# Attention and two gated FFNs on one core: state products on half-array rows, attention on small tiles, and x loaded by ScalarE's queue

## The chip, the core and the metric

The kernel runs on one core of a Trainium2 chip. The time is the device time of one execution in microseconds; smaller is better. Three executions before the change gave 1411.93, 1411.97 and 1413.6 us, a median of 1411.97 us. A profiled execution of the same program took 1415.93 us.

## The reference, cut to what matters

```python
# x[8, 8, 512, 64], state[8, 8, 32, 64]: batch, head, row, feature
scores = x @ state.T / 8;   a  = softmax(scores)    # rows of x over 32 state rows
xread  = a @ state
scores2 = state @ x.T / 8;  a2 = softmax(scores2)   # state rows over 512 rows of x
sread  = a2 @ x
t = concat([xread, sread], rows)      # per batch 512 + 32 rows, 8 heads x 64 = 512 columns
t = t.transpose(0, 2, 1, 3).reshape(4352, 512)
h = ((t @ w1) * (t @ w2)) @ w3 @ w_out              # 512 -> 1024 -> 1024 -> 512
y = (sigmoid(h @ w_gate) * (h @ w_val)) @ w_out2    # 512 -> 1536 -> 512
```

Everything is float32. w_gate is scaled by 200, so the argument of the sigmoid is large and the products must be precise. The weights arrive as 64-bit floats and are converted on the chip from their two 32-bit halves.

## The kernel before, in words

**Precise products.** An operand is split into two fp32r parts (a rounded one and the rest), and a product takes three matmuls: high by high, high by low, low by high (`products`, L103 to L115). The attention's own small products (scores, state read, transposes) are plain fp32 matmuls; each shows two records in the trace.

**State products.** For the 512 rows of a batch, xread @ w1 is a @ (state @ w1). The kernel computes state @ w1 and state @ w2 per head ("state products", `sw_step`, L337), stores them in DRAM (sw_d, tile swd) and reads them back per batch as weights (`sw_weights`, L458: swf is the loaded tile, swh its two parts). For this, `bd` holds the transposed state as a block diagonal: 128 rows are two heads of 64 features, and the columns of a head are zero in the other head's rows. A step multiplies one 128x512 piece of a weight (wh) with two blocks of bd's parts (bds): six matmuls of 128 rows and 512 columns into two PSUM banks (psw), two copies by ScalarE, one store. 16 steps for four of the batches stand at the start, 16 for the other four in the stages t = 1 and 2.

**Stages.** `ffn1` (L408) runs once per batch, t = 0 to 7 (the batches in the order 0, 4, 1, 5, 2, 6, 3, 7), and once more for the state rows. A stage has eight steps j (groups pab: a @ swh for w1 and w2; ScalarE copies the first to asb, VectorE multiplies, both split the result to u) and four steps d (groups py: u times wp, the product of w3 and w_out, which stage 0 computes). Before each step the functions in its slot run, in the order in which the lists are filled (L610 to L645). By them the attention of the next batch is laid into the stage:

- slots 6 and 7: four groups of transposes of x (xn to PSUM tile pxt to xT, L166 to L173);
- slot 8: the scores (tile psc), and from it both softmaxes; slot 9: the rest of the first one, which gives aT, the operand of the next stage;
- in the next stage, slots 1 and 2: transposes of the second softmax (pa2); slot 4: the state read (`sread`, tile psr, copied to sr with the normalisation); slot 6: its transposes (`sreadt`, tile psrt, copied to xst).

`load_x` (L152) issues eight DMAs, one per head, on SyncE in slot 0 of the stage (slot 7 for t = 0). Its buffer comes alternately from two pools, one buffer each. From stage 3 on, the preparation of the second FFN's weights (raw, w_gate, w_val) also stands in slots.

**What sets the order.** The order of TensorE's instructions is the order of the program (L147: `manual_schedule` for PE). The order on the other engines is made by a scheduler. PSUM has eight banks: four for pab and psw (L128), two for py, two for everything of the attention.

**The rest.** The stage of the state rows ends at 620 us; the second FFN, which the change does not touch, runs to the end.

Of the kernel before, what the change touches and what calls it, by code (L numbers as in the profile page):

```python
# [20 lines left out]
def tile_state_attention__then__gated_ffns(  # L21
# [96 lines left out]
    sw_d = dram.tile([2, 2, 2, 2, P, B // 2, 512], F32, name="swd")  # L118
# [19 lines left out]
    bd = keep.tile([P, G, B // 2, P], F32, name="bd")  # L138
# [7 lines left out]
    with tc.manual_schedule(engines={mybir.EngineType.PE}):  # L146
# [5 lines left out]
        def load_x(b, pool):  # L152
            t = pool.tile([P, G, SC, 2, D], F32, name="xn", bufs=1)
            for h in range(H):
                nc.sync.dma_start(
                    out=t[:, h // 2, :, h % 2], in_=x[b, h].rearrange("(p c) d -> p c d", c=SC)
                )
            xn[b] = t

        def attention(b):  # L160

            b2, bp = divmod(b, B // 2)
# [14 lines left out]
            def scores():  # L177
# [5 lines left out]
                for k in range(2):  # L183
                    pt = ps_at.tile([P, 512], F32, tag="at", name="psc")
                    for q in range(2):
                        nc.tensor.matmul(
                            pt[64 * q : 64 * q + 64],
                            bd[:, 2 * k + q, bp, b2 * 64 : b2 * 64 + 64],
                            t["xT"][:, 2 * k + q],
                            start=True,  # L190
                            stop=True,
                        )
                    nc.vector.transpose(out=t["st"][:, k].rearrange("p a n -> p (a n)"), in_=pt)
# [46 lines left out]
            def sread():  # L240
                pt = ps_at.tile([P, 2, P], F32, tag="at", name="psr")
                for k in range(2):
                    for c in range(SC):
                        for q in range(2):
# [7 lines left out]
                t["sr"] = at.tile([P, 2, P], F32, name="sr")  # L252
# [5 lines left out]
            def sreadt():  # L258
                pt = ps_at.tile([P, 2, 2, 2, NS], F32, tag="at", name="psrt")
                for k in range(2):  # L260
# [3 lines left out]
                xv = p2["xst"].rearrange("p (k q) n -> p k q n", q=2)  # L264
                for h2 in range(2):
                    nc.vector.tensor_copy(
                        out=xv[64 * h2 : 64 * h2 + 64, :, :, b * NS : (b + 1) * NS],
                        in_=pt[64 * h2 : 64 * h2 + 64, :, :, h2],
                    )
# [865 lines left out]
```

## Time and profile before

| quantity | value |
|---|---|
| median of three executions | 1411.97 us |
| profiled execution | 1415.93 us |
| its span, first to last instruction | 1414.2 us |
| mean granted clock of TensorE | 0.983 |
| TensorE busy | 1343.5 us, 95% |
| VectorE busy | 924.7 us, 65% |
| ScalarE busy | 750.2 us, 53% |
| GpSimd busy | 278.3 us, 20% |

Times in the profile run from the start of the span, 1.7 us less than the execution. Busy is the time in which an engine has an instruction under way; a step that stands beside others on an engine that is busy throughout is seen by the distance of its start to the next one's, not by its mean. The granted clock is 1 for full speed. The stages lie at 75 to 194.9 us (t = 0), 194.9 to 257.6, 257.6 to 321.5, 321.5 to 373.2, 373.2 to 424.9, 424.9 to 483.3, 483.3 to 535 and 535 to 586 us (t = 7), then the state rows; these bounds were read from the timeline as the first pab of each stage.

### The profile page before, as it was taken

How to read it: one execution, taken by the hardware profiler on the slowest of the kernel's cores; microseconds unless marked ns; L12 is line 12 of the kernel's file. 1: busy time of each engine (PE TensorE's matmuls, PEld its weight loads, DVE VectorE, ACT ScalarE, POOL GpSimd, SP SyncE). 2: the span in 40 equal slices, each digit the busy share in tenths (PEclk: the TensorE clock that was granted, in tenths of full speed). 3: DMA queues.
4: the chain of work that ended last, by engine and by line, in shares of the span. 5: the costliest groups of instructions: out<-in, count | busy, mean ns of one | idle time of the engine just before them, and what ended most of it. 6: DMA issues, size and time to landing. Idle time of an engine off the chain costs nothing.

```text
span 1414.2 us, 18988 instructions
## 1 busy us (share of the span) xinstructions
PE 1343.5 (95%) x6560; PEld 1145.6 (81%) x6560; DVE 924.7 (65%) x1523; ACT 750.2 (53%) x1480; POOL 278.3 (20%) x255
## 2 busy tenths in 40 slices
PE   5669999999998999999999999999999999999997
PEld 3348877777876777898988998988988888988996
DVE  6789756645555566528677667778777677556543
ACT  6877656756445456436546546545545544433421
POOL 2352113324334234001121121021121110000000
PEclk9889999999999999999999999999999999999999
DMA  9867637754446354383343347655445694134132
GB/s 264 290 195 212 199 135 230 228 195 127 138 119 164 90 155 152 118 319 116 133 151 100 117 165 285 239 183 169 136 167 184 227 324 159 62 108 137 49 104 67
DMA packets 169128, 237.18 MB, mean 168 GB/s; under 512 B 46920, under 2 KB 111944, under 8 KB 166984
## 3 DMA queue, kind: packets, MB, share of 16 engines
q1 hardware_dynamic: 130536, 163.15, 36.6%
q10 hardware_dynamic: 37344, 63.39, 12.8%
q0 software_dynamic: 1152, 9.44, 1.9%
q8 instruction: 51, 0.84, 0.2%
q14 instruction: 45, 0.37, 0.1%
HBM read 150.99 MB, written 84.93 MB: 167 GB/s over the span
## 4 chain that ended last, share of the span: by engine, by line
PE 80%; DVE 6%; issue 5%; DMA 4%; POOL 2%; ACT 2%; ACTq 0%; SPq 0%; DVEq 0%; POOLq 0%
PE po L1019 19%; PE psA L922 18%; PE psB L922 9%; PE pab L112 8%; PE py L112 7%; PE psC L922 5%; PE pab L115 4%; PE py L115 4%; DMA yf<-yd 2%; PE pwp L112 2%; POOL wh L66 2%; PE pwp L115 1%; PE psr L245 1%; PE pxt L170 1%; DMA raw<-in_moe_w 1%
## 5 line engine op out<-in xcount | busy, mean ns | idle before, releaser
L922 PE MATMUL psA<-y,wt 128*128 128x448 f32 (+1 forms) x1440 | 304.6, 360 | 5.6 <-ACT u L61 2.8
L922 PEld LDWEIGHTS psA<-y,wt 128*128 128x128 f32 x1440 | 266.3, 188 | 25.8 <-ACT u L61 3.9
L1019 PE MATMUL po<-wo,p 128*128 128x512 f32 x1224 | 280.7, 389 | 0.4 <-DVE p L590 0.4
L1019 PEld LDWEIGHTS po<-wo,p 128*128 128x128 f32 x1224 | 229.5, 188 | 48.3 <-DVE p L590 1.0
L922 PE MATMUL psB<-y,wt 128*128 128x448 f32 (+1 forms) x720 | 161.1, 359 | 0.0
L66 POOL TENSOR_TENSOR o<-m,o 128x256 fp32r<-128x256 f32 x72 | 59.3, 823 | 503.3 <-ACT o L61 449.1
L112 PE MATMUL pab<-aT,swh 128*128 128x512 f32 x512 | 145.7, 407 | 12.2 <-ACT asb L61 4.7
L922 PEld LDWEIGHTS psB<-y,wt 128*128 128x128 f32 x720 | 133.5, 188 | 8.5
L112 PE MATMUL py<-u,wp 128*128 128x512 f32 (+1 forms) x576 | 132.2, 381 | 2.1 <-DVE u L66 1.7
L61 ACT ACTIVATE u<-psA 128x448 f32<-128x448 f32 (+1 forms) x120 | 63.9, 532 | 127.7 <-PE psA L922 103.0
L112 PEld LDWEIGHTS py<-u,wp 128*128 128x128 f32 x576 | 104.0, 189 | 28.5 <-issue 5.7
L66 POOL TENSOR_TENSOR swh<-swf,swh 128x512 fp32r<-128x512 f32 x64 | 90.8, 1424 | 167.9 <-ACT swh L61 155.0
L112 PEld LDWEIGHTS pab<-aT,swh 128*128 128x128 f32 x512 | 95.3, 193 | 35.0 <-ACT asb L61 6.4
L61 ACT ACTIVATE p<-sg 128x448 fp32r<-128x448 f32 (+1 forms) x120 | 67.9, 566 | 86.6 <-DVE sg L958 79.0
L434 DVE TENSOR_TENSOR asb<-asb,pab 128x512 f32<-128x512 f32 (+1 forms) x72 | 47.0, 654 | 98.8 <-PE pab L115 90.3
L101 DVE CUSTOM_DVE_ANT_0 m<-m,r 128x1024 uint16<-128x1024 uint16 (+1 forms) x116 | 80.1, 692 | 11.1 <-ACT r L90 1.3
L66 DVE TENSOR_TENSOR u<-asb,u 128x512 fp32r<-128x512 f32 (+1 forms) x72 | 65.9, 916 | 30.7 <-ACT u L61 30.1
L1034 DVE TENSOR_TENSOR ob<-po,ob 128x512 f32<-128x512 f32 x68 | 46.8, 688 | 58.7 <-PE po L1019 55.4
L115 PE MATMUL pab<-aT,swh 128*128 128x512 f32 x256 | 81.7, 401 | 2.0 <-POOL swh L66 2.0
L922 PE MATMUL psC<-y,wt 128*128 128x448 f32 (+1 forms) x360 | 80.9, 360 | 1.1 <-DVE s L955 1.1
L61 ACT ACTIVATE y<-yf 128x448 fp32r<-128x448 f32 (+1 forms) x120 | 63.1, 558 | 32.4 <-DMA yf<-yd 32.4
L98 DVE SCALAR_TENSOR_TENSOR m<-raw,m 128x512 uint32<-128x512 uint32 (+1 forms) x116 | 78.2, 676 | 3.2
(118 smaller groups left out, 2028.3 us busy)
## 6 DMA issues: line engine op xcount, KB each, us to landing
raw<-in_moe_w SPq DMA_DIRECT2D x48, 512.0 KB, 5.6
wt<-wd SPq DMA_DIRECT2D x12, 1792.0 KB, 7.6
part<-ob SPq DMA_DIRECT2D x68, 256.0 KB, 2.8
ob<-part SPq DMA_DIRECT2D x68, 256.0 KB, 3.9
yf<-yd SPq DMA_DIRECT2D x37, 448.0 KB, 4.0
swd<-swst ACTq DMA_DIRECT2D x32, 512.0 KB, 4.1
swf<-swd SPq DMA_DIRECT2D x128, 128.0 KB, 3.7
wd<-o ACTq DMA_DIRECT2D x56, 256.0 KB, 2.3
```

Source lines behind the costliest of these rows:

```text
L61: return nc.scalar.activation(out=o, in_=i, func=AF.Copy)
L66: (sub or nc.vector).tensor_tensor(out=lo, in0=src, in1=hi.bitcast(F32), op=ALU.subtract)
L98: nc.vector.scalar_tensor_tensor(out=mu, in0=hi, scalar=0x80000000, in1=mu, op0=ALU.bitwise_and, op1=ALU.bitwise_or)
L101: nc.vector.tensor_tensor(out=m.bitcast(I32), in0=m.bitcast(I32), in1=r, op=ALU.add)
L112: nc.tensor.matmul(o, w[i], xx[k], start=n == 0 and i + k == 0, stop=False)
L115: nc.tensor.matmul(o, w[1 - late], xx[late], start=False, stop=n == len(pairs) - 1)
L170: nc.tensor.transpose(pt[:, c * P : (c + 1) * P], xn[b][:, g, c].rearrange("p a d -> p (a d)"), ident)
L245: nc.tensor.matmul(pt[64 * q : 64 * q + 64, k], t["a2"][:, k, c, 64 * q : 64 * q + 64], xn[b][:, 2 * k + q, c].rearrange("p a d -> p (a d) ...
L434: p2["dve"] = nc.vector.tensor_tensor(out=asb[:, :n], in0=asb[:, :n], in1=pab[1][:, :n], op=ALU.mult)
L922: nc.tensor.matmul(o, w[:, i, kb * P : (kb + 1) * P], xx[kb][h], start=start, stop=i == 1 and kb == 1, skip_group_check=True,)
L1019: nc.tensor.matmul(o, pt[j][i][:, s * P : (s + 1) * P], wot[j][:, h], start=j == js[0] and i + h == 0, stop=j == js[-1] and i == 1,)
L1034: nc.vector.tensor_tensor(out=ob, in0=o, in1=ob, op=ALU.add)
```

## The change

**State as it is.** The zero blocks go. z holds the state of four batches side by side (128 rows = 4 batches x 32), and one transpose per pair of heads turns it into stT: 64 rows per head, 128 columns for four batches. The first four batches are now 0 to 3, the order of the batches is 0 to 7, and the second half is turned after the fourth step of the start.

**State products.** Each of the six matmuls of a step uses the 64 rows of one head (the other head's matmul the other 64), both write all 128 columns of output, in two PSUM banks; the order is pair by pair.

**Scores and state read.** The scores become eight matmuls of 64 rows and 32 columns of output instead of four of 128 rows and 64. The state read becomes 32 matmuls, each for one head (32 output columns, 64 elements), instead of 16 for two heads each (64 columns, 128 elements, half of which were not used). Its result is turned with one transpose instead of two and copied with one copy instead of two.

**Loads.** swf is read with one DMA instead of two. x of a batch is loaded by ScalarE's queue, in slot 8 of the stage two before its own, behind the scores' place, instead of SyncE's in slot 0 of the stage one before; the first two batches stay on SyncE.

```diff
-    bd = keep.tile([P, G, B // 2, P], F32, name="bd")
+    stT = keep.tile([P, G, NSR], F32, name="stT")
...
         def load_x(b, pool, queue=nc.sync):
...
# scores
-                        nc.tensor.matmul(
-                            pt[64 * q : 64 * q + 64],
-                            bd[:, 2 * k + q, bp, b2 * 64 : b2 * 64 + 64],
-                            t["xT"][:, 2 * k + q],
+                pts = [ps_at.tile([P, 512], F32, tag="at", name="psc") for _ in range(2)]
+                for g in range(G):
+                    for k in range(2):
+                        nc.tensor.matmul(
+                            pts[k][NS * g : NS * g + NS],
+                            stT[64 * k : 64 * k + 64, g, b * NS : (b + 1) * NS],
+                            t["xT"][64 * k : 64 * k + 64, g],
...
# sread
-                        for q in range(2):
+                        for g in range(G):
                             nc.tensor.matmul(
-                                pt[64 * q : 64 * q + 64, k],
-                                t["a2"][:, k, c, 64 * q : 64 * q + 64],
-                                xn[b][:, 2 * k + q, c].rearrange("p a d -> p (a d)"),
+                                pt[NS * g : NS * g + NS, k],
+                                t["a2"][:, k, c, NS * g : NS * g + NS],
+                                xn[b][:, g, c, k],
...
# sreadt
-                for k in range(2):
-                    nc.tensor.transpose(
-                        pt[:, k].rearrange("p q h n -> p (q h n)"), t["sr"][:, k], ident
-                    )
-                for h2 in range(2):
-                    nc.vector.tensor_copy(
...
+                nc.tensor.transpose(
+                    pt.rearrange("p g n -> p (g n)"), t["sr"].rearrange("p k d -> p (k d)"), ident
+                )
+                nc.vector.tensor_copy(out=p2["xst"][:, :, b * NS : (b + 1) * NS], in_=pt)
...
# the start
-        nc.vector.memset(z, 0.0)
+        for b in range(B):
+            (nc.sync if b in (1, 3) else nc.scalar).dma_start(
+                out=z[b % 4 * NS : b % 4 * NS + NS, b // 4],
...
# sw_step
-            products(*[(po[q], [([t[:, g, q] for t in bds], wh)]) for q in range(2)], late=1)
+            for m, (x, w) in enumerate(((0, 0), (1, 0), (0, 1))):
+                for k in range(2):
+                    nc.tensor.matmul(
+                        po[k],
+                        sts[x][64 * k : 64 * k + 64, g],
+                        wh[w][64 * k : 64 * k + 64],
...
-        order = [q * (B // 2) + bp for bp in range(B // 2) for q in range(2)]
+        order = list(range(B))
...
# the stages
-                slots[7 if t == 0 else 0].insert(
-                    0, lambda t=t: load_x(order[t + 1], at if t % 2 else pu)
-                )
+                if t == 0:
+                    slots[7].insert(0, lambda: load_x(order[1], pu))
+                if t + 2 < B:
+                    slots[JF].append(
+                        lambda t=t: load_x(order[t + 2], pu if t % 2 else at, nc.scalar)
+                    )
```

On TensorE, in the stage t = 1, the state read and the first step of the state products stand between the step j = 3 and j = 4. aT and swh are the operands of pab, bds and sts the two parts of the state. Before:

```order
L115 MATMUL pab<-aT_1665,swh_1737 128x512 x2
L245 MATMUL psr<-xn,a2tr 64x128 x16
L112 MATMUL psw<-wh_1819,bds_1487 128x512
L112 MATMUL psw<-wh_1819,bds_1488 128x512
L112 MATMUL psw<-wh_1819,bds_1487 128x512
L112 MATMUL psw<-wh_1819,bds_1488 128x512
L115 MATMUL psw<-wh_1820,bds_1487 128x512 x2
L112 MATMUL pab<-aT_1665,swh_1770 128x512
```

And after the change, at the same place:

```order
L115 MATMUL pab<-aT_1676,swh_1738 128x512 x2
L246 MATMUL psr<-xn,a2tr 32x64 x32
L344 MATMUL psw<-wh_1819,sts_1490 128x512 x2
L344 MATMUL psw<-wh_1819,sts_1491 128x512 x2
L344 MATMUL psw<-wh_1820,sts_1490 128x512 x2
L112 MATMUL pab<-aT_1676,swh_1770 128x512
```

The place in TensorE's order is the same; the state read has twice the matmuls of half the size, and the six matmuls of the step now stand as three pairs, one for each head.

On SyncE's queue before, around the start of the stage t = 5, the eight loads of x stand behind ten loads of swf:

```order
L465 DMA swf<-swd 64x4x128 x4
L80 DMA raw<-in_moe_w_gate 128x4x256
L465 DMA swf<-swd 64x4x128 x2
L80 DMA raw<-in_moe_w_gate 128x4x256
L465 DMA swf<-swd 64x4x128 x10
L155 DMA xn<-in_x 128x4x64 x8
L465 DMA swf<-swd 64x4x128 x4
```

After the change they stand on ScalarE, in the stage t = 4 among others, behind the copies of the state read (sr):

```order
L255 ACTIVATE sr<-psr,r_3355 128x64 x2
L155 DMA xn<-in_x 128x4x64 x2
L61 ACTIVATE asb<-pab 128x512
L155 DMA xn<-in_x 128x4x64 x2
L61 ACTIVATE u_3724<-asb 128x512
L61 ACTIVATE asb<-pab 128x512
L155 DMA xn<-in_x 128x4x64 x2
L61 ACTIVATE u_3751<-asb 128x512
L61 ACTIVATE xT<-pxt 128x512 x2
L155 DMA xn<-in_x 128x4x64
```

The loads of x have left SyncE's queue. On ScalarE they are spread among the copies of pab (asb), the conversions to u and the copies of the transposed x.

## Rows read from the trace of the kernel before

**Rows 1.** Busy line of the page (engine, us, share, instructions).

```profile
PE 1343.5 (95%) x6560; PEld 1145.6 (81%) x6560; DVE 924.7 (65%) x1523; ACT 750.2 (53%) x1480; POOL 278.3 (20%) x255
```

**Rows 2.** Table by stage: us; busy PE, PEld, DVE, ACT, POOL; clock, DMA share.

```profile
0.00:75.00 75.00, 42.92 (x136) 26.17 (x136) 51.08 (x73) 56.53 (x105) 23.47 (x22) 0.86 0.87 277
...
194.90:257.60 62.70, 61.97 (x308) 49.69 (x308) 38.96 (x53) 42.95 (x78) 22.18 (x16) 1.00 0.61 188
...
373.20:424.90 51.70, 50.96 (x260) 40.76 (x259) 30.89 (x43) 27.89 (x51) 18.41 (x16) 1.00 0.43 123
424.90:483.30 58.40, 52.51 (x260) 41.99 (x259) 33.26 (x43) 28.13 (x50) 18.52 (x16) 0.94 0.50 140
...
586.00:1414.20 828.20, 811.81 (x4033) 729.41 (x4032) 548.34 (x987) 393.78 (x833) 90.70 (x104) 1.00 0.47 161
```

**Rows 3.** Timeline of TensorE, one step of the state products (start us, us).

```profile
205.01 1.07 PE L112 MATMUL psw<-wh,bds 128*128 128x512 f32 x4
205.92 0.61 PE L115 MATMUL psw<-wh,bds 128*128 128x512 f32 x2
206.37 1.07 PE L112 MATMUL pab<-aT,swh 128*128 128x512 f32 x4
```

**Rows 4.** Groups by shape, score products (busy us, mean ns).

```profile
L186 PE MATMUL psc<-xT,bd 128*64 128x512 f32 x64 | 15.5, 605 | 0.4 <-ACT xT L61 0.4
```

**Rows 5.** Timeline of TensorE, scores in one stage, state read in the next.

```profile
348.83 0.61 PE L115 MATMUL pab<-aT,swh 128*128 128x512 f32 x2
349.38 1.94 PE L186 MATMUL psc<-xT,bd 128*64 128x512 f32 x8
351.24 0.74 PE L112 MATMUL py<-u,wp 128*128 128x512 f32 x2
...
385.08 1.97 PE L245 MATMUL psr<-xn,a2tr 128*64 128x128 f32 x32
386.98 0.73 PE L112 MATMUL pab<-aT,swh 128*128 128x512 f32 x2
```

**Rows 6.** Timeline, turning the state read and the next transposes of x.

```profile
340.90 0.38 PE L261 MATMUL psrt<-ident,sr 128*128 128x128 f32 x2
...
341.77 0.58 DVE L266 COPY xst<-psrt 64x128 f32<-64x128 f32 x2
...
342.46 0.63 PE L170 MATMUL pxt<-ident,xn 128*128 128x128 f32 x4 [0.74 <-PE pxt L170]
```

**Rows 7.** Timeline of SyncE's queue, 405 to 451 us.

```profile
406.21 37.69 SPq L465 DMA_DIRECT2D swf<-swd  x10
443.95 6.26 SPq L155 DMA_DIRECT2D xn<-in_x  x8
```

**Rows 8.** Timeline of TensorE at 451 us, and the table over that stretch.

```profile
450.95 1.09 PE L170 MATMUL pxt<-ident,xn 128*128 128x128 f32 x4 [5.89 <-issue]
...
447.50:454.40 6.90, 3.45 (x11) 2.92 (x12) 4.03 (x5) 1.54 (x3) 1.69 (x2) 0.51 1.02 248
```

**Rows 9.** Timeline, TensorE waiting at the end of stage 0.

```profile
196.00 0.53 PEld L112 LDWEIGHTS pab<-aT,swh 128*128 128x128 f32 x3 [1.07 <-DVE aT L66]
```

**Rows 10.** Timeline of GpSimd, two of the steps at the start.

```profile
46.46 1.42 POOL L66 TENSOR_TENSOR wh<-m,wh 128x512 fp32r<-128x512 f32 x1 [2.64 <-ACT wh L61]
...
53.15 1.41 POOL L66 TENSOR_TENSOR wh<-m,wh 128x512 fp32r<-128x512 f32 x1 [2.64 <-ACT wh L61]
```

**Rows 11.** Groups by shape, the memset of z, ScalarE's copies of bds, bd, sr.

```profile
L286 DVE MEMSET z<- 128x2048 f32 x1 | 1.8, 1765 | 1.2 <-PEq L1117 1.2
L61 ACT ACTIVATE bds<-bd 128x256 fp32r<-128x256 f32 x8 | 2.8, 414 | 0.0
L61 ACT ACTIVATE bd<-pt 128x512 f32<-128x512 f32 x4 | 2.3, 601 | 0.5 <-PE pt L299 0.5
L254 ACT ACTIVATE sr<-psr,r 128x128 f32<-128x128 f32 x16 | 4.9, 360 | 1.5 <-PE psr L245 1.5
```

**Rows 12.** Instructions on tile xn: the issues (ns min/median/max, first and last start).

```profile
L155 SPq DMA_DIRECT2D xn<-in_x x64: 539/629/1767, 6.9 to 449.4; - x64
```

More of the change, by code (lines that the diff above doesn't have):

```diff
@@ L335, in sw_prep, with state_split, sw_step @@
             return ahead(prep, 2, 2 * JF)
[L337 to L347 removed]
+        def state_split(pool, h4):
+            t = [pool.tile([P, G, P], F32R, name=f"sts{i}", bufs=1) for i in range(2)]
+            for g in range(G):
+                v = [i[:, g].rearrange("p (n b) -> p b n", b=4) for i in t]
+                split(*v, stT[:, g, h4 * P : (h4 + 1) * P].rearrange("p (b n) -> p b n", b=4))
+            return t
+        def sw_step(i, h4, sts, wh, pool):
+            hf, g, a = sw_tile(i)
+            st = pool.tile([P, 2, 512], F32, name="swst", bufs=3 if h4 == 0 else 2)
+            po = [ps_main.tile([P, 512], F32, tag="m", name="psw") for _ in range(2)]
+            for m, (x, w) in enumerate(((0, 0), (1, 0), (0, 1))):
+                for k in range(2):
+                    nc.tensor.matmul(
+                        po[k],
+                        sts[x][64 * k : 64 * k + 64, g],
+                        wh[w][64 * k : 64 * k + 64],
+                        start=m == 0,
+                        stop=m == 2,
+                    )
+            for k in range(2):
+                copy("act", st[:, k], po[k])
+            nc.scalar.dma_start(
+                out=sw_d[h4, hf, g, :, :, a].rearrange("n b k f -> (n b) (k f)"),
+                in_=st.rearrange("p k f -> p (k f)"),
+            )
+        order = list(range(B))
         before, after = attention(order[0])
[L349 removed]
+        sts = state_split(p1, 0)
         wh = sw_prep(p1, (cv, p1), False)
@@ L354, in tile_state_attention__then__gated_ffns @@
         for i in range(2 * JF):
-            sw_step(i, 0, bds, wh(i), p1)
+            sw_step(i, 0, sts, wh(i), p1)
             if i == 0:
@@ L463, in prep @@
                 f0 = j % 4 * P
-                for q in range(2):
-                    nc.sync.dma_start(
-                        out=f[64 * q : 64 * q + 64].rearrange("p k a f -> p (k a) f"),
-                        in_=sw_d[
-                            j // 4, q, :, :, 64 * b2 : 64 * b2 + 64, bp, f0 : f0 + P
-                        ].rearrange("k a p f -> p (k a) f"),
-                    )
+                nc.sync.dma_start(
+                    out=f.rearrange("p a k f -> p (a k) f"),
+                    in_=sw_d[b // 4, j // 4, :, :, b % 4, :, :, f0 : f0 + P].rearrange(
+                        "g n a k f -> (g n) (a k) f"
+                    ),
+                )
                 t = [
@@ L475, in prep @@
                 split(t[0], t[1], f, sub=nc.gpsimd)
-                return [[t[i][:, :, a] for i in range(2)] for a in range(2)]
+                return [[t[i][:, a] for i in range(2)] for a in range(2)]
             return ahead(prep, 2, JF)
```

75 lines of the change are left out of this document (27 added, 48 removed).

## The prediction

> **What bounds the kernel now.** I read the page's busy line first, then the table by stage, then the timeline of single stages, then the groups by shape. The busy line says that TensorE is busy for 95% of the span [rows 1], so an edit pays where it takes TensorE work away or a wait out of TensorE's order. The table by stage says where each holds [rows 2]. Up to 75 us TensorE is busy for 42.9 of 75 us; ScalarE sets the pace there. In the stages of the later batches TensorE is full: 0.7 us idle in the one from 194.9 us and in the one from 373.2 us. The stage from 424.9 us is the exception: 58.4 us long against 51.7 us for its neighbour with the same work, with a granted clock of 0.94. From 586 us on the work is untouched by the change; I count nothing there.
>
> The long stage has one wait in it. SyncE spends 406.21 to 443.90 us on ten issues of swf, because each must wait for a buffer, and the eight loads of x stand behind them in the same queue; they are issued from 443.95 to 450.21 us [rows 7]. TensorE's next transpose of that x starts at 450.95 us after 5.89 us of idling, and from 447.5 to 454.4 us the clock is half (0.51) [rows 8].
>
> **State products (L344 after, L112/L115 before).** A step is six 512-column matmuls: 205.01 to 206.37 us, 1.36 us, 0.227 us each [rows 3]. Now each uses 64 of the 128 rows, the two of a pair lie on different halves of the array and in different PSUM banks, so three slots of 0.227 us remain if a pair runs together: 0.68 us. No row shows two row halves together. What rows show is column halves together: the eight records of a score product have a mean of 605 ns but fill 1.94 us, 2.5 at a time [rows 4, 5]. Entering such a shape costs 0.10 us (the pair at 348.83 us is followed after 0.55 us, the one at 205.92 after 0.45), leaving it 0.09 us (351.24 lies 0.08 us before the scores' end at 351.32, a normal successor 0.16 us before, 206.37 against 206.53) [rows 3, 5]. So a step costs 0.68 + 0.19 = 0.87 us instead of 1.36. Bounds: no overlap, +0.19; overlap and no drain, -0.68. I take -0.49, the shape nearest in the rows. Only the 16 steps in the stages from 194.9 and 257.6 us are on TensorE's path: **-7.8 us** (bounds +3.0 and -10.9). The 16 at the start lie beside ScalarE's pace.
>
> **Scores (L185 after, L186 before).** Four matmuls, eight records, run in four slots of two: 349.38 to 351.24 us less 0.1 for leaving, 0.44 us a slot [rows 5]. Now there are eight matmuls and 16 records; eight tiles at once make two slots, -0.88 us; four at once four slots, 0; two at once eight slots, +1.8. I take two slots, since both tiles that stood open before were used. Six stages count; in stage 0 the end of this chain is late already (the first matmul after 194.9 us waits 1.07 us for aT [rows 9]), so there the gain turns into a longer wait. 6 x -0.88 = **-5.3 us** (bounds 0 and, over seven batches, +12.6).
>
> **State read (L246 after, L245 before).** 16 matmuls, 32 records, take 1.90 us [rows 5], 1.8 without leaving, 0.113 us per pair. Now 32 matmuls of 64 columns: 64 records of half the length. Four at once: 16 slots of 0.056, -0.9 us; two at once: 32 slots, 0. The densest that a row shows is these 32 records in 1.90 us. I take two thirds, -0.6, since four tiles at once also asks for twice the records and weight loads per time. 8 x -0.6 = **-4.8 us** (bounds -7.2 and +1.6).
>
> The Trainium skill ("TensorEngine Tiling (Array Packing)", Performance Considerations, Instruction Overhead) speaks against this edit: a matmul costs some 60 cycles however few columns it has, and a tiling factor is not to be taken from a dimension that is small already. At 2.4 GHz, as an estimate from that page, 64 records would take 1.6 us, and the term would be -1.6 us instead of -4.8; no row here packs records closely enough to test it.
>
> **Turning the state read (L261, L266).** One transpose instead of two, and one copy of the result instead of two in 0.58 us. The second transpose of x must wait for a PSUM buffer until these copies end at 342.35 us, and starts at 342.46 [rows 6]. Half the copies, 0.29 us, goes in the four stages from 321.5 us that have no state product in between; the transpose, 0.1 us of the two's 0.38, goes in all eight. 4 x -0.29 - 8 x 0.1 = **-2.0 us** (bounds 0 and -3).
>
> **x on ScalarE's queue.** x of a batch is issued in the stage before, behind the state read that frees its buffer, so the wait of the long stage goes: 58.4 - 51.7 = **-6.7 us**, the cold clock included [rows 2, 8]. What is late next there is the wait for a PSUM buffer (above) that the neighbours have as well. SyncE loses 48 issues of x and half of the swf issues. ScalarE gains them: 48 x 0.629 us = 30 us of issuing [rows 12], 5 us per stage. In the stage from 194.9 us ScalarE is busy 42.95 of 62.7 us [rows 2], so the time is there, but its order is strict: queued behind an issue are the next copy of pab, u, xT and e. Such a copy has slack (PSUM holds two more groups of 1.36 us, 2.7 us), 0.63 us fits, two do too; an issue that itself waits for an earlier transfer on SyncE doesn't. I take **+1.5 us** (bounds 0 and +15, half of all issues bare).
>
> **Start.** The 1.76 us memset of z goes [rows 11], the loads of state stand first in two queues, 16 transposes become four and four more later. On ScalarE bd's four copies of 601 ns and four of bds's of 414 become two of about 600 and four of about 360 (the nearest 128x128 copy, sr) [rows 11]: 4.1 to 2.6 us, -1.5. The start's steps come in pairs 6.69 us apart (46.46 to 53.15) [rows 10], which doesn't change. ScalarE's first instruction is now the copy of the transposed state, in front of the first conversion. If state lands late this holds all up, by about 2 us; if it lands early, up to 2 us of ScalarE's early gaps go as well. I take **-2.0 us** (bounds +2 and -4).
>
> **Sum.** -7.8 - 5.3 - 4.8 - 2.0 - 6.7 + 1.5 - 2.0 = -27.1 us. The profiled execution took 1415.9 us (span 1414.2 and 1.7 around it), so 1388.8 us; the median of the runs, 1412.0, lies 3.9 us below the profiled one, so 1385 us.
>
> **Rivals.**
> 1. Row halves don't run together: the state products cost +3.0 instead of -7.8, the scores 0 instead of -5.3: 1385 + 16.1 = 1401 us. For: no row shows row halves together. Against: column halves do.
> 2. The state read is paced by its records, not its columns: +0.2 instead of -0.6 a batch: 1385 + 6.4 = 1391 us. For: 64 records and 64 weight loads where 32 took 1.9 us. Against: 32 took no longer than their columns. The skill's rule on instruction overhead (above) is a milder form of this.
> 3. The change doesn't do what it says: x is still late, or the wait moves to ScalarE, whose x issues wait for older swf transfers on SyncE and hold up pab's copies. Without the 6.7 us and with 5 us of new stalls: 1397 us. For: SyncE held swf up for 37.7 us [rows 7]. Against: x has more than half a stage to spare.
> 4. Slower: the small tiles run one after the other. Scores 16 x 0.44 = 7.0 us, +5.3 in each of seven batches; state read 64 x 0.056 = 3.6, +1.8 in each of eight; products +3.0: 37.1 + 14.4 + 3.0 = +54.5, less the 9.2 of the four other terms (-2.0 - 6.7 - 2.0 + 1.5): 1412 + 45 = 1457 us. It decides from the point where the three terms lose more than those 9.2 us, about 1.1 us a batch. Against: pairs overlapped before.
>
> **How the numbers follow.** Forecast 0.58 (its own range 1376 to 1393), rival 1 0.12, rival 2 0.12, rival 3 0.12, rival 4 0.06. The range 1374 to 1402 takes in all but rival 4 and the tails. A measurement of this kernel can't tell 0.2% (2.8 us) from no change. All but rival 4 are faster by more than that; I leave 0.04 for a mixture that cancels. Faster 0.90, same 0.04, slower 0.06.
>
> **What would show it.** Products: six records in about 0.7 us, starting in pairs. Scores: from 1.86 to about 1.0 us. State read: 1.9 to about 1.3. The stage of the sixth batch as long as its neighbours, no stretch at half clock in it. x's issues on ScalarE's queue at 0.6 us each, without a wait of TensorE for pab's copies behind them. Wrong would be: stages from 321.5 us no shorter than 51 us, or new idle time of TensorE before pab.

## The result and the profile after

The kernel after the change takes 1395.95 us (median of four runs, 1391.33 to 1397.8), against 1411.95 us for the kernel before in the same comparison (four runs): a ratio of 0.9883, 95% interval 0.9855 to 0.991, or 16.0 us less. The forecast was 1385 us with a range of 1374 to 1402; the sign is right, the range holds, and the gain is 11 us smaller than forecast. The profiled executions differ by 20.6 us: 1395.35 against 1415.93 us. In later comparisons the kernel before had medians from 1413.1 to 1415.8 us.

The first thing to look at is where the stages begin (the first pab of each in the timeline). This table is made from both timelines:

| stretch, us | before | after | difference | forecast |
|---|---|---|---|---|
| start | 75.0 | 81.2 | +6.2 | -2.0 |
| t = 0 | 119.85 | 120.14 | +0.3 | -0.7 |
| t = 1 and 2 | 126.63 | 115.71 | -10.9 | -11.0 |
| t = 3, 4 and 6, each | 51.67 | 49.62 | -2.05 | -1.9 |
| t = 5 | 58.43 | 50.18 | -8.25 | -8.6 |
| t = 7 | 51.10 | 49.72 | -1.4 | -0.7 |
| ScalarE's issues of x, all stages | | | not visible | +1.5 |
| state rows, second FFN | 828.1 | 827.8 | -0.3 | 0 |

All stages with the changed arithmetic came out within a microsecond of the forecast; the start alone missed by 8.2 us. Of t = 0 and t = 7 these two executions tell little: among the kernels below that change nothing there, t = 0 takes 120.1 to 122.3 us and t = 7 47.9 to 50.4. The lines of after that answer to [rows 1] and [rows 2] are these: the busy line, and the table by stage (columns: PE, PEld, DVE, ACT, POOL busy, granted clock, DMA share, GB/s).

```profile
PE 1318.1 (95%) x6864; PEld 1115.4 (80%) x6864; DVE 913.7 (66%) x1514; ACT 745.1 (53%) x1478; POOL 281.0 (20%) x255
```

```profile
0.00:81.20 81.20, 37.85 (x136) 17.79 (x137) 49.90 (x72) 55.36 (x103) 24.11 (x22) 0.71 0.80 255
...
201.30:259.80 58.50, 57.71 (x346) 43.12 (x347) 32.75 (x48) 38.17 (x71) 18.17 (x14) 1.00 0.58 183
366.60:416.20 49.60, 49.09 (x298) 39.51 (x298) 29.70 (x42) 27.22 (x51) 18.85 (x16) 1.00 0.46 138
416.20:466.40 50.20, 49.17 (x299) 39.55 (x298) 30.63 (x42) 28.25 (x50) 19.29 (x16) 1.00 0.54 163
...
600.30:1393.60 793.30, 777.93 (x3746) 694.83 (x3745) 534.76 (x959) 378.77 (x801) 91.30 (x104) 1.00 0.46 157
```

TensorE is busy 25 us less, and its share of the span is the same 95%. In the first 81.2 us it is busy for 37.9 us at a mean clock of 0.71, where before it was 42.9 of 75 us at 0.86 (the clock's records begin at 27.5 and 14.1 us; ahead of them the table counts 1.00): the start did not become shorter with its work.

What the three small products cost now is in the timeline of TensorE; the rows answer to [rows 3] and [rows 5]. First a step of the state products, then a state read that stands directly in front of a step, then the scores.

```profile
211.16 0.61 PE L115 MATMUL pab<-aT,swh 128*128 128x512 f32 x2
211.71 0.97 PE L344 MATMUL psw<-wh,sts 64*128 64x512 f32 x6
212.60 1.20 PE L112 MATMUL pab<-aT,swh 128*128 128x512 f32 x4
...
215.55 1.10 PE L246 MATMUL psr<-xn,a2tr 128*32 128x64 f32 x64
216.58 0.96 PE L344 MATMUL psw<-wh,sts 64*128 64x512 f32 x6
```

```profile
343.18 0.61 PE L115 MATMUL pab<-aT,swh 128*128 128x512 f32 x2
343.73 1.09 PE L185 MATMUL psc<-xT,stT 64*32 64x512 f32 x16
344.75 0.50 PE L112 MATMUL py<-u,wp 128*128 128x512 f32 x1
```

A step takes 0.89 us (211.71 to 212.60) instead of 1.36. The scores' 16 records fill 1.02 us (343.73 to 344.75) instead of 1.86 with eight, the state read's 64 records 1.03 us instead of 1.90 with 32. Turning the state read, before the second transposes of x may start, takes 1.21 us, where [rows 6] had 1.56:

```profile
335.56 0.27 PE L261 MATMUL psrt<-ident,sr 128*128 128x128 f32 x1
...
336.77 0.66 PE L169 MATMUL pxt<-ident,xn 128*128 128x128 f32 x4 [0.51 <-DVE xst L264]
```

x's loads stand where the change puts them, 16 on SyncE and 48 on ScalarE (columns: ns min/median/max, first and last start); they answer to [rows 12].

```profile
L155 ACTq DMA_DIRECT2D xn<-in_x x48: 547/604/1800, 115.2 to 442.3; - x48
L155 SPq DMA_DIRECT2D xn<-in_x x16: 540/628/2359, 3.7 to 110.0; - x16
```

### The profile page after: what moved, and what is told of

Same layout as the page of the kernel before. It is cut to its first block, busy times and chain, and to the rows that moved or that the text cites. A ratio compares the mean times of both kernels' runs of the same rounds, so it can differ in the third digit from the quotient of the medians.

```text
span 1393.6 us, 19413 instructions
## 1 busy us (share of the span) xinstructions
PE 1318.1 (95%) x6864; PEld 1115.4 (80%) x6864; DVE 913.7 (66%) x1514; ACT 745.1 (53%) x1478; POOL 281.0 (20%) x255
## 4 chain that ended last, share of the span: by engine, by line
PE 80%; DVE 6%; DMA 5%; issue 4%; ACT 2%; POOL 1%; SPq 0%; ACTq 0%; DVEq 0%; POOLq 0%
PE po L1032 18%; PE psA L935 18%; PE psB L935 9%; PE py L112 8%; PE pab L112 8%; PE psC L935 5%; PE py L115 4%; PE pab L115 4%; DMA yf<-yd 2%; PE pwp L112 1%; DMA ob<-part 1%; POOL wh L66 1%; PE psw L344 1%; DMA raw<-in_moe_w 1%; PE pxt L169 1%
## 5 line engine op out<-in xcount | busy, mean ns | idle before, releaser
L89 ACT ACTIVATE m<-raw 128x512 f32<-128x512 f32 (+1 forms) x116 | 65.7, 567 | 29.3 <-POOL o L66 15.6
```

The lines of the kernel that those rows point to most:

```text
L89: nc.scalar.activation(out=m, in_=hi.bitcast(F32), func=AF.Abs, scale=2.0**-112)
```

## The experiments

Each kernel was run four to ten times beside the kernel before. The table gives stretches of the profiled executions, since t = 3, 4 and 6 repeat to a hundredth of a microsecond and t = 1 and 2 to some tenths where a kernel changes nothing in them. The start repeats to 0.7 us (80.7 to 81.4 in the five kernels that leave it as after the change has it), and the second FFN, which no kernel changes, varies by 4 us between executions, so spans alone tell little under that.

| kernel | start | t = 1, 2 | t = 3 | t = 5 | second FFN | ratio to before, interval |
|---|---|---|---|---|---|---|
| before | 75.0 | 126.6 | 51.67 | 58.43 | 793.5 | 1 |
| after | 81.2 | 115.7 | 49.61 | 50.18 | 793.2 | 0.9883 (0.9855 to 0.991) |
| z_half | 81.9 | 115.7 | 49.62 | 50.71 | 790.5 | 0.9864 (0.9836 to 0.9892) |
| prod_serial | 80.7 | 115.9 | 49.62 | 50.21 | 792.0 | 0.9861 (0.9836 to 0.9887) |
| scores_rows | 81.4 | 116.0 | 49.62 | 50.18 | 792.5 | 0.9851 (0.9823 to 0.9879) |
| x_sp | 80.7 | 117.0 | 49.61 | 49.61 | 791.6 | 0.9866 (0.9843 to 0.9889) |
| z_pool | 79.3 | 115.7 | 49.61 | 53.43 | 791.9 | 0.9898 (0.9874 to 0.9922) |
| prod_same_half | 81.2 | 126.8 | 49.61 | 50.15 | 792.5 | 0.9948 (0.9929 to 0.9966) |
| before_xst | 75.5 | 126.7 | 51.16 | 55.30 | 791.9 | 0.997 (0.9956 to 0.9984) |
| before_x | 75.5 | 124.8 | 51.67 | 55.66 | 790.4 | 0.9974 (0.9963 to 0.9985) |
| raw_first | 79.5 | 115.7 | 49.62 | 53.29 | 791.3 | 0.9893 (0.9876 to 0.9909) |
| turn_early | 80.9 | 115.7 | 48.95 | 48.95 | 790.9 | 0.9828 (0.9814 to 0.9843) |
| before_turn | 75.0 | 130.0 | 50.77 | 53.92 | 792.3 | 0.9955 (0.9941 to 0.9969) |
| turn_z_pool | 79.9 | 115.8 | 48.95 | 48.95 | 789.5 | 0.9838 (0.9817 to 0.9858) |

### Do the halves and tiles run together?

**prod_same_half**: both matmuls of a pair on the same half.

```diff
-                        sts[x][64 * k : 64 * k + 64, g],
-                        wh[w][64 * k : 64 * k + 64],
+                        sts[x][0:64, g],
+                        wh[w][0:64],
```

> Both matmuls of each pair of the state products use the rows of the same half (the second head's products are therefore left out). Theory (the gain comes from two halves running at once): six slots of 0.227 us instead of three, +0.68 us a step, the stages t = 1 and 2 together 10.9 us longer than 115.7 us, 1407 us. Rival (half the rows make a matmul cheaper by themselves): no change, 115.7 us and 1396 us.

Measured: t = 1 and 2 take 11.05 us longer, and the median is 1404.71 us. The step shows it directly:

```profile
212.96 1.66 PE L344 MATMUL psw<-wh,sts 64*128 64x512 f32 x6
214.55 1.19 PE L112 MATMUL pab<-aT,swh 128*128 128x512 f32 x4
```

1.59 us instead of 0.89, so 0.70 us a step. The gain is the two halves running at once; half the rows alone gain nothing.

**prod_serial** and **scores_rows**: only the order of the loops.

```diff
# prod_serial
-            for m, (x, w) in enumerate(((0, 0), (1, 0), (0, 1))):
-                for k in range(2):
+            for k in range(2):
+                for m, (x, w) in enumerate(((0, 0), (1, 0), (0, 1))):
# scores_rows
-                for g in range(G):
-                    for k in range(2):
+                for k in range(2):
+                    for g in range(G):
```

> The six matmuls of a step of the state products in another order: three of the one row half, then three of the other. Theory (halves run together only where their matmuls stand side by side in the order): 5 or 6 slots of 0.227 us instead of 3, so a step takes 0.45 to 0.68 us longer, the stages t = 1 and 2 together 7 to 11 us longer than 115.7 us, and 1403 to 1407 us. Rival (TensorE looks past a waiting matmul to one for a free half): no change, 1396 us.

> The eight matmuls of the scores in another order: four of the one row half, then four of the other. Theory (as for the products, tiles run together only if they stand side by side and are all free): the two times four tiles of 32 columns run one group after the other, 1.9 us instead of 1.02, in six stages +5 us, 1401 us. Rival (eight tiles start within 0.05 us in the trace, so the issue is fast against a tile's 0.42 us, and both orders fill all eight): no change, 1396 us.

Measured: t = 1 and 2 together changed by 0.2 us, and the medians are 1395.31 and 1395.96 us. My theory that the halves must alternate in the program's order fell in both. The step of prod_serial takes 0.90 us:

```profile
212.68 0.97 PE L344 MATMUL psw<-wh,sts 64*128 64x512 f32 x6
213.58 0.73 PE L112 MATMUL pab<-aT,swh 128*128 128x512 f32 x2
```

Its six matmuls start at 212.68, 212.69, 213.01, 213.02, 213.25 and 213.26 us, in pairs. In the built program they still stand three and three, and the second weight load to start in the trace carries the wait that the program gives to the other half's first matmul. So it is TensorE that brings the halves together, as the rival had it.

### What was the 5.89 us wait?

**x_sp**: x loaded as before the change, all else after it.

```diff
-                if t == 0:
-                    slots[7].insert(0, lambda: load_x(order[1], pu))
-                if t + 2 < B:
-                    slots[JF].append(... load_x(order[t + 2], pu if t % 2 else at, nc.scalar))
+                slots[7 if t == 0 else 0].insert(
+                    0, lambda t=t: load_x(order[t + 1], at if t % 2 else pu)
+                )
```

> x loaded as before the change: by SyncE's queue, in slot 0 of the stage before (slot 7 for t = 0); all else as after the change. Theory (the queue change is worth the late x of one stage): a stage of about 56 to 57 us comes back among the 49.6 us ones, and +6.7 us, 1403 us. Rival (SyncE has half as many loads of swf now, so x would be in time there as well): +0 to 2 us, 1396 to 1398 us.

Measured: 1396.91 us, and no long stage: t = 5 takes 49.61 us with SyncE's loads. The queue of x is not what removed the long stage. So I read the stage of the kernel before again, this time the timelines of SyncE, TensorE and VectorE and of GpSimd around the wait (start us, us).

```profile
389.52 5.33 SPq L155 DMA_DIRECT2D xn<-in_x  x8
```

```profile
502.88 0.60 PE L170 MATMUL pxt<-ident,xn 128*128 128x128 f32 x4
```

```profile
444.97 0.69 DVE L434 TENSOR_TENSOR asb<-asb,pab 128x512 f32<-128x512 f32 x1 [1.18 <-ACT asb L61]
446.36 3.39 DVE L66 TENSOR_TENSOR u<-asb,u 128x512 fp32r<-128x512 f32 x1 [0.69 <-ACT u L61]
449.68 0.67 DVE L434 TENSOR_TENSOR asb<-asb,pab 128x512 f32<-128x512 f32 x1
450.27 0.58 DVE L266 COPY xst<-psrt 64x128 f32<-64x128 f32 x2
451.05 0.69 DVE L66 TENSOR_TENSOR u<-asb,u 128x512 fp32r<-128x512 f32 x1 [0.19 <-ACT u L61]
```

```profile
446.70 2.50 POOL L66 TENSOR_TENSOR swh<-swf,swh 128x512 fp32r<-128x512 f32 x2
```

The x that the waiting transposes read was issued from 389.52 us, 55 us earlier, a group of eight loads in the stage before. The loads at 443.95 us [rows 7], which the prediction took for it, fill the other buffer and are read from 502.88 us in the next stage. TensorE waited for a PSUM buffer. The attention has two; psrt holds one of them until VectorE has copied it to xst, and that copy stood behind a multiplication, a subtraction of 3.39 us and another multiplication in VectorE's order. It ended at 450.85 us; the transposes started at 450.95 [rows 8]. The next subtraction of the same shape takes 0.69 us (451.05); the long one ended 0.56 us after GpSimd's two subtractions had.

**before_xst**, **before_x** and **before_turn** test this on the kernel before, each with one edit: the copy to xst on ScalarE; x on ScalarE's queue as after the change; the turning one step earlier, so that one step j (two groups of pab) lies between it and the transposes, where before there was none.

```diff
# before_xst, in sreadt
-                    nc.vector.tensor_copy(
+                    nc.scalar.activation(
...
# before_x, in the stages
-                slots[7 if t == 0 else 0].insert(
-                    0, lambda t=t: load_x(order[t + 1], at if t % 2 else pu)
-                )
+                if t == 0:
+                    slots[7].insert(0, lambda: load_x(order[1], pu))
+                if t + 2 < B:
+                    slots[JF].append(... load_x(order[t + 2], pu if t % 2 else at, nc.scalar))
# before_turn
-            after = {1: [lambda: a2t(0)], 2: [lambda: a2t(1)], 4: [sread], 6: [sreadt]}
+            after = {1: [lambda: a2t(0)], 2: [lambda: a2t(1)], 4: [sread], 5: [sreadt]}
...
```

> The kernel before the change, with the copy of the turned state read (xst) on ScalarE instead of VectorE. Theory (the 5.89 us wait of TensorE in the stage from 424.9 us is for the PSUM buffer that this copy frees, since the copy stands on VectorE behind a subtraction of 3.39 us that ran while GpSimd's two subtractions ran; x, issued 55 us earlier, was there): the stage of 58.4 us shrinks to about 52 us, the kernel by 6 to 7 us. Rival, the prediction's reading (x comes late): the stage stays at 58.4 us.

> The kernel before the change, with x loaded by ScalarE's queue half a batch sooner, as after the change, and nothing else of it. The prediction's reading (x comes late in the stage from 424.9 us): that stage shrinks from 58.4 to 51.7 us, 6.7 us faster than before. Theory now (x was in time): no gain from x itself; the stage is long or short by where VectorE's copy and GpSimd's subtractions fall, and the other stages stay at 51.7 us, or grow by ScalarE's issues, 0 to 2 us in all.

> The kernel before the change, with the turning of the state read one step j earlier and nothing else; x is loaded by SyncE as before. Theory (the 5.89 us wait in the stage from 424.9 us, and smaller ones of its neighbours, are for the PSUM buffer that VectorE's copy frees): that stage shrinks from 58.4 to 51 us or less, its neighbours by about 0.7 us, 9 to 11 us faster than before. The prediction's reading (x comes late): that stage stays at 58 us; only the neighbours gain, about 3 us in all.

Measured: the excess of the stage t = 5 over t = 3 was 6.8 us before; it is 4.1 us in before_xst (t = 3, 4 and 6 are 0.5 us shorter as well), 4.0 us in before_x and 3.2 us in before_turn. Each takes a part and none removes it whole, so the stage of 52 us that I expected of before_xst did not come: 55.3 us lies halfway between my theory and its rival. The rows of TensorE's wait in before_xst and before_x, and in before_turn where it is spread over three places:

```profile
448.74 1.12 PE L170 MATMUL pxt<-ident,xn 128*128 128x128 f32 x4 [2.78 <-ACT xst L266]
```

```profile
449.39 0.79 PE L170 MATMUL pxt<-ident,xn 128*128 128x128 f32 x4 [3.11 <-issue]
```

```profile
444.82 0.59 PE L261 MATMUL psrt<-ident,sr 128*128 128x128 f32 x2 [0.35 <-ACT sr L254]
...
448.96 0.63 PE L170 MATMUL pxt<-ident,xn 128*128 128x128 f32 x4 [0.36 <-PE pxt L170]
...
454.44 0.66 PE L170 MATMUL pxt<-ident,xn 128*128 128x128 f32 x4 [1.66 <-ACT xT L61]
```

The rest is more of the same. In before, 5.2 of the 6.8 us are waiting beyond the 0.74 us of t = 3, and 1.6 us are the half clock [rows 8]. In before_xst and before_x TensorE still waits 2.6 and 2.4 us longer than in t = 3, and 3.4 us at half clock behind the wait cost 1.6 us. In before_turn it waits 2.4 us in all, at full clock.

In before_x the wait is still there with x loaded sooner, and it is shorter because GpSimd's subtractions fell elsewhere: VectorE's subtraction in front of the copy takes 0.69 us there. In before_xst and before_turn the long subtraction is still there (3.39 and 3.46 us), but the copy no longer stands behind all of it. My expectation of 9 to 11 us for before_turn was too high: t = 2 grew by 3.2 us in it, where TensorE now waits 2.4 us for ScalarE's copy asb and 0.9 us for VectorE's product, instead of 1.3 us in all.

A long subtraction is thus not needed for a long wait. In the kernel after the change, and in z_pool below, which differs from it only in the start, VectorE's product, subtraction, product and copy xst in t = 5 take 2.87 us in both. First VectorE in after, where TensorE starts the turning (psrt) at 434.79 us, then in z_pool, where it starts it at 433.71 us:

```profile
433.59 0.69 DVE L447 TENSOR_TENSOR asb<-asb,pab 128x512 f32<-128x512 f32 x1 [1.18 <-PE pab L115]
...
436.18 0.28 DVE L264 COPY xst<-psrt 128x128 f32<-128x128 f32 x1
```

```profile
434.21 0.69 DVE L447 TENSOR_TENSOR asb<-asb,pab 128x512 f32<-128x512 f32 x1 [1.18 <-ACT asb L61]
...
436.80 0.28 DVE L264 COPY xst<-psrt 128x128 f32<-128x128 f32 x1
```

The turning falls 1.20 us behind the first product's start in after and 0.50 us ahead of it in z_pool, and the waits are 1.03 and 2.73 us. What makes VectorE late in this stage is probably the conversion of a piece of w_out2 (wot): ScalarE stands idle in front of it, 2.15 and 1.62 us, until VectorE has made its operand (m), and the copy of pab that the product needs stands behind it. It starts 0.4 to 2.4 us ahead of the turning in t = 5 of all kernels that turn in slot 6; in t = 4 and 6 it lies 8 us or more away, and t = 3 has none. No run moved it, so this last link is read from rows only.

**turn_early** is the same move in the kernel after the change.

```diff
-            after = {1: [lambda: a2t(0)], 2: [lambda: a2t(1)], 4: [sread], 6: [sreadt]}
+            after = {1: [lambda: a2t(0)], 2: [lambda: a2t(1)], 4: [sread], 5: [sreadt]}
...
             for i, fns in after.items():
-                slots[i + 2 if t == 0 else i] += fns
+                slots[8 if t == 0 and i == 5 else i + 2 if t == 0 else i] += fns
```

> The turning of the state read (psrt, xst) stands one step j earlier (slot 5 instead of 6, in stage 0 as it was); all else as after the change. Theory (the second transpose of x waits 0.5 us in most stages, 1.0 us in the stage from 416.2 us, for the PSUM buffer that VectorE's copy xst frees): these waits go, the stages t = 3, 4 and 6 take 49.1 instead of 49.6 us, t = 5 as well instead of 50.2, about 3 us in all, 1393 us. Rival (the state read's copies by ScalarE are not done one step after it): TensorE waits for sr before the transpose instead, same or longer stages, 1396 us or more.

Measured: 1389.09 us (1388.11 to 1390.51), the lowest median of this study; its interval lies wholly below that of after. No wait for the PSUM buffer is left, and t = 3 to 6 take 48.95, 48.93, 48.95 and 48.93 us, 3.3 us less in all. Its profiled span is 7.3 us shorter than that of after; t = 7 and the second FFN gave 2.3 us each, about what executions vary by there.

```profile
431.37 0.27 PE L261 MATMUL psrt<-ident,sr 128*128 128x128 f32 x1
...
434.24 1.03 PE L169 MATMUL pxt<-ident,xn 128*128 128x128 f32 x8
```

### Why did the start become longer?

In the kernel after the change these rows stand out: ScalarE's first issues, x's loads on SyncE, what these waited for, a wait of ScalarE, and the table for 10 to 20 us, before and after.

```profile
0.74 4.89 ACTq L282 DMA_DIRECT2D z<-in_state  x6
...
20.11 0.66 ACT L89 ACTIVATE m<-raw 128x512 f32<-128x512 f32 x1 [4.86 <-DMA raw<-in_moe_w]
```

```profile
3.74 11.32 SPq L155 DMA_DIRECT2D xn<-in_x  x8
```

```profile
SPq L155 <- DMA z<-in_state: 5.0, 4, 3.3
```

```profile
10.00:20.00 10.00, 7.74 (x40) 6.43 (x42) 4.54 (x10) 9.06 (x20) 4.04 (x3) 1.00 1.00 224
```

```profile
10.00:20.00 10.00, 3.92 (x14) 2.35 (x14) 6.43 (x8) 3.61 (x6) 3.27 (x2) 1.00 0.95 211
```

ScalarE issues six of the eight loads of state, for 4.89 us, before its first copy. SyncE's loads of x wait 5.0 us for transfers of state, of which x needs nothing, and take 11.32 us instead of 6.52 us in before. The fourth weight piece stands behind x; its conversion stands in ScalarE's order in front of the copies of xT, and ScalarE waits 4.86 us for it. From 10 to 20 us ScalarE is busy 3.61 us instead of 9.06. Three kernels change the loads:

```diff
# z_half: batches 4 to 7 only after the first step's first copy, by ScalarE
+                with tc.issue_after(p2_act[0].ins):
+                    for b in range(B // 2, B):
+                        load_z(b)
# z_pool: batches 4 to 7 by GpSimd's queue
-            (nc.sync if b in (1, 3) else nc.scalar).dma_start(
+            (nc.gpsimd if b >= 4 else nc.sync if b in (1, 3) else nc.scalar).dma_start(
# raw_first: queues as in z_pool, batches 4 to 7 after the first step's first copy as in z_half,
# and three weight pieces first
+        wh(0)
+        for b in range(B // 2):
+            load_z(b)
+        state_turn(0)
```

> The state of batches 4 to 7 is loaded only after the first step's first copy; all else as after the change. Theory (loads of x wait for the eight loads of state ahead of them: 5.0 us in SyncE's queue, and the fourth weight piece stands behind x): SyncE's loads of x then take about 6.5 us instead of 11.3, ScalarE's first conversion comes about 1 us sooner, and the first pab starts at about 76 us instead of 81.2: 1391 us against 1396. Rival (the start is longer because TensorE runs at half clock there, its work having become less): first pab stays at 81 us, 1396 us.

> The state of batches 4 to 7 is loaded by GpSimd's queue instead of ScalarE's; all else as after the change. In the run with the second half of state loaded late by ScalarE, its loads held ScalarE for 6.6 us, so that run did not separate the causes. Theory (the start is longer because loads of state stand in front of other work in ScalarE's and SyncE's queues): no issue of state then waits on ScalarE, x's loads take about 7 to 9 us instead of 11.3, first pab at about 76 us instead of 81.2, 1391 us. Rival (half clock of TensorE from 36 to 78 us sets it): first pab stays at 81 us, 1396 us.

> The first three weight pieces are asked for before the state, as in the kernel before, and the state of batches 4 to 7 by GpSimd's queue; all else as after the change. Theory (ScalarE sets the pace of the start, and after the change it is idle for 5.5 us more than before between 10 and 20 us, since weight pieces land later and their conversions stand in its order in front of the copies of xT): ScalarE is busy from 10 to 20 us for 7 us or more instead of 3.6, and the first pab starts at 75 to 77 us instead of 81.2: 1390 us. Rival (the half clock of TensorE): busy time may change, the first pab stays at 79 to 81 us, 1394 to 1396 us.

Measured: first pab at 81.9, 79.3 and 79.5 us; medians 1395.89, 1396.96 and 1397.93 us. z_half replaced one wait by another of its kind: ScalarE was held by the late issues of state, and its copies of xT behind them:

```profile
17.10 6.63 ACTq L282 DMA_DIRECT2D z<-in_state  x3
23.77 1.08 ACT L61 ACTIVATE xT<-pxt 128x512 f32<-128x512 f32 x2 [6.52 <-DMA z<-in_state]
```

With four of the six issues of state off ScalarE, 1.7 to 1.9 us of the 6.2 came back; the theory expected 4 to 6. The loads of x did not recover with it: in z_pool none of them waits for state any more, and they still take 10.92 us (8.66 in raw_first, 9.43 in z_half, where 7 to 9 and 6.5 were expected of z_pool and z_half). So the wait for state alone does not make them long. In raw_first ScalarE was busy 5.42 us from 10 to 20 us, not the 7 expected: it waits for weight pieces and for step 1. The half clock did not set the pace either. From 51 us on the steps come in pairs 6.67 us apart, as before [rows 10], and TensorE waits for ScalarE in each pair:

```profile
61.83 1.22 PE L344 MATMUL psw<-wh,sts 64*128 64x512 f32 x4 [1.77 <-ACT wh L61]
...
68.50 1.22 PE L344 MATMUL psw<-wh,sts 64*128 64x512 f32 x4 [1.77 <-ACT wh L61]
```

The pace is the same at either clock: from 60 to 70 us the granted clock is 0.50 (1.2 GHz) in after; in before it is 1.00 (2.4 GHz), and the steps at 59.81 and 66.51 us are 6.70 us apart.

The time is lost early: the first step starts at 14.10 us instead of 13.74, the second at 27.52 instead of 21.44, the last at 75.16 instead of 69.27. Between the first two TensorE has the first batch's transposes and scores. Their second half and the second step, before and then after:

```profile
18.03 1.14 PE L170 MATMUL pxt<-ident,xn 128*128 128x128 f32 x8 [1.42 <-ACT xT L61]
...
21.44 1.21 PE L112 MATMUL psw<-wh,bds 128*128 128x512 f32 x4
```

```profile
22.80 1.97 PE L169 MATMUL pxt<-ident,xn 128*128 128x128 f32 x8 [4.32 <-ACT xT L61]
...
27.52 3.09 PE L344 MATMUL psw<-wh,sts 64*128 64x512 f32 x18
```

Of the 6.1 us lost by the second step, 4.8 lie in front of these transposes, where TensorE waits for ScalarE's copies of xT, and 1.3 in the transposes and scores, which take 4.7 us instead of 3.4, since TensorE is slower there (these eight transposes take 1.97 us instead of 1.14). So the rival has a small part in it. In z_pool the two parts are 3.2 and 0.9 us. The five kernels nearly agree in one thing: the later the first batch's scores start, the later the first pab (19.57 and 75.0 us before; 22.66 and 79.5 in raw_first; 23.15 and 79.3 in z_pool, the one pair out of order; 24.70 and 81.2 after; 26.52 and 81.9 in z_half). That is a correlation. What still holds z_pool and raw_first back by some 4.3 us, with the issues of state off ScalarE, stays open.

Neither kernel gained in its median, because z_pool and raw_first lost in t = 5 what they won in the start: 53.4 and 53.3 us instead of 50.2. Nothing in that stage was changed. The wait for the PSUM buffer is 2.73 us long there instead of 1.03 us in after, and behind it the clock is half:

```profile
437.14 0.65 PE L169 MATMUL pxt<-ident,xn 128*128 128x128 f32 x4 [2.73 <-DVE xst L264]
```

```profile
438.00:440.00 2.00, 2.00 (x7) 1.56 (x6) 0.27 (x1) 0.43 (x1) 0.00 (x0) 0.51 0.89 242
```

```profile
436.52 0.66 PE L169 MATMUL pxt<-ident,xn 128*128 128x128 f32 x4 [1.03 <-DVE xst L264]
```

**turn_z_pool** puts turn_early and z_pool together (no other edit).

> After the change, with the turning one step earlier and the state of batches 4 to 7 on GpSimd's queue. Theory (in the run with GpSimd's queue alone, 1.9 us of the start were won and 3.2 us lost again to the PSUM buffer in the stage t = 5, a wait that the earlier turning removes): first pab at about 79.3 us, stages t = 3 to 6 at 48.95 us, 1387 us against 1389 with the earlier turning alone. Rival (the two are not independent, or the start's gain is given back later): 1389 us or more.

Measured: 1390.61 us (1386.1 to 1392.63), not distinguishable from turn_early, with the shortest profiled span, 1384.3 us. So the rival held for the median: a gain in the start is not seen in it. The stages t = 3 to 6 are at 48.9 us; the first pab stands at 79.9 us, 1.1 us ahead of turn_early, where z_pool was 1.9 us ahead of after.

## Why the prediction was right and wrong

**State products: the mechanism was right, the size was not.** Halves run together (prod_same_half). The term was -7.8 us for 16 steps. Adding up the distances between TensorE's starts in t = 1 and 2, the products took 5.9 us less. The mis-sized number is the cost of entering and leaving the shape: I took 0.19 us a step, and it is 0.39, since on each side two distances grow, that to the next shape's first matmul (0.32 instead of 0.23 us) and the one after it (0.33 instead of 0.23). That holds for a step between two groups of full shape, which gains some 0.25 us; a step beside the state read, a transpose or the scores gains 0.3 to 0.5, since it shares a change of shape with its neighbour. The two stages still came out at -10.9 us as forecast, since a wait of TensorE for asb, 1.3 us in t = 2, went as well, which I had not counted. In the view of TensorE's waits of before (us in total, times, longest):

```profile
PE pab L112 <- ACT asb L61: 1.3, 1, 1.3
```

**Scores: right.** 0.84 us a stage instead of 0.88; eight tiles run at once, each record 613 ns, 16 of them in 1.02 us.

**State read: right, too small.** -0.87 us instead of -0.6; all four column tiles run at once. The 64 records start 14 ns apart on average. The Trainium skill's rule that I set against it ("TensorEngine Tiling (Array Packing)", Instruction Overhead; as an estimate 1.6 us for these records) does not show here: 1.03 us. Rival 2, paced by records, is refuted by the same row.

**Turning: right in size.** 0.35 us less from the turning to the second transposes of x. What I did not draw from the same rows [rows 6] is that the wait left over, 0.5 us and more in each stage, could be removed by one position in the order (turn_early).

**The long stage: right size, wrong cause.** The step "the eight loads of x stand behind them in the same queue", and with it the wait, failed. [rows 7] and [rows 8] stand 1 us apart in time, and I took the one for the cause of the other without asking which buffer those loads fill. x_sp has x on the old queue and no long stage; before_x has x on the new queue and still a stage 4.0 us too long. The wait was for VectorE's copy out of PSUM. That the change shortened it came from where the instructions of VectorE, ScalarE and GpSimd fell against the turning; z_pool and raw_first moved them a little and got 3.1 to 3.3 us back into the stage. The term was luck.

**x on ScalarE's queue: +1.5 us forecast, a gain measured.** No wait of TensorE for ScalarE's copies of pab appears after the change in t = 1 to 7, and before_x keeps t = 3, 4 and 6 at 51.67 us. The queue alone is worth 1.3 us in t = 2 (58.5 us in x_sp, 57.3 after) or 1.9 us (63.9 before, 62.0 in before_x): the wait for asb above is there only with x on SyncE. Why SyncE's loads bring it about was not followed up. Rival 3's first half, that x's new place doesn't do what it says, is true in its way: x was never late.

**Start: -2.0 us forecast, +6.2 measured.** This is the step that cost the forecast most of its 11 us. I counted ScalarE's copies and did not ask what the new loads stand in front of: six issues in ScalarE's order before its first conversion, and x's loads behind transfers of state. I had named a late state as a risk of 2 us, and bounded the term at +2. The runs give some 1.9 of the 6.2 us to the issues of state on ScalarE. The rows put the loss between the first step and the second, 4.8 us of it in front of ScalarE's copies of xT; which load holds these once the issues are gone is not shown. The turning of the second half of the state, which stands behind the fifth step and not the fourth, comes after the loss.

**The median: 4.5 us of the 11.** The profiled execution of before lay 3.9 us above its median, that of after 0.6 us below. Carrying the one offset over to the other was a guess. The rest adds up so: 8.2 us of the start and 4.5 us here, less 1.7 us by which all other terms together came out better.

## What to carry to other kernels

When a wait ends shortly after a transfer starts, check which buffer that transfer fills and who reads it, before calling it the cause; here two PSUM buffers, the strict order of VectorE and ScalarE and, before the change, GpSimd's subtractions made the wait, and one position in TensorE's order (turn_early) removed it in t = 3 to 6. When an edit moves loads to the front of a program, count what each new issue stands in front of in its queue. A shape change on TensorE costs on both sides: put enough work between, and halves or small tiles that run at once pay for it.

## What the runs showed of the hardware

- Matmuls of the two row halves start together even when the program has three of the one half and then three of the other: the starts are in pairs 0.01 us apart, and a step takes 0.90 us in prod_serial, 0.89 after.
- A subtraction of VectorE took 3.39 us beside two subtractions of GpSimd that ran back to back (446.70 to 449.20 us), instead of 0.69; one beside a single subtraction of GpSimd (441.35 to 442.64 us) took 1.36. The Trainium skill ("SBUF — State Buffer", SBUF: two separate sides) says that the two engines share a port pair that one of them holds for its whole instruction while the other is blocked. The trace agrees as far as it goes: the subtraction ended 0.56 us after the second of them; but it began 0.34 us before the first, so the start times do not show who held the pair.
- A wait of TensorE of 2.73 us was followed by a granted clock of 0.51 (1.2 GHz) from 438 to 440 us; one of 1.03 us at the same place was followed by none. So 1.7 us more of waiting cost 3.2 us of stage. In before_xst, before_x and raw_first waits of 2.78, 3.11 and 2.89 us were followed by half clock too, in z_half one of 1.58 us was not.
